# Another order of the first loads, and other transfers for h and D, in a kernel of a long convolution and a gated MLP

## The chip, the core and the metric

The kernel runs on one core of one Trainium2 chip. The core has a matrix engine (TensorE, PE in the profile; its weight loads are listed as PEld), a vector engine (VectorE, DVE), a scalar engine (ScalarE, ACT), GpSimd (POOL) and SyncE (SP), which here issues nearly all transfers. Every engine works through its own instructions in order and waits at semaphores for the others. The transfers themselves run on 16 DMA engines. The metric is device time in microseconds (us), lower is better: a median of 234.15 us over 3 runs before the change (233.83 to 234.19).

## The reference

One input x (2048 rows of 640) is normalised, and two branches of it are added to it:

```python
xn = layernorm(x)
# branch A: a short and a long convolution along the rows, gated by xn
k_shift = sum over t < 4 of (k shifted down by t rows) * shift_k[:, t]
kv = k_shift * v
y  = causal convolution of kv with ssm_k (length 2048 per column, by FFT) + kv * ssm_D
A  = xn * y
# branch B: a gated MLP of width 1728
h  = sigmoid(xn @ w_gate) * (xn @ w_up)
B  = h @ w_down
out = x + A + B
```

The data are bf16. In what follows h is the convolution's filter `A_ssm_k` (640 x 2048), not the MLP's hidden layer, which is called `hT`. D is `A_ssm_D`, 640 values.

## The kernel before

**Branch B** goes in four passes t of 512 rows, `xn` transposed in `xnT`. A pass makes 13 blocks of 128 hidden columns (5 matmuls of 512 columns for gate, 5 for up, L271), a 14th half block (L292), and then the product with the down weights `wd` (L315), in which each output tile takes 14 matmuls in two halves of 7. ScalarE makes the sigmoid (L280), VectorE the product into `hT` (L286), and VectorE adds the output to x (L320).

**Branch A** goes in five chunks c of 128 columns. The convolution is a transform in two stages, by matmuls with tables. For a chunk, VectorE makes kv from four shifted copies of k and the taps `sc` (`kv_op`, L348 to L357), and it brings the filter into the layout of kv by a transpose in 32 x 32 blocks (`h_turn`, L334, two per chunk, each over all 128 partitions of `hn`). D is added to the filter's first row by GpSimd (`add_D`, L328). Stage 1 are the matmuls L374 and L376, which write to `ps`; their results go through DRAM to be rearranged (L392 writes, L409 reads); stage 2 is L418; then come the products L431 and L433, and the way back (L447, L463, L479, L488). At the end `inv2_q` (L493) multiplies by xn into the small buffer `yx` and `inv2_x` (L498) adds it to x.

**Layernorm** of the rows of passes 1 to 3 (groups g) is made on the way: statistics (L200, L204), a power on GpSimd (L212), the normalised tile (L217 on VectorE, L229 on ScalarE). x of group 1 comes by `load_x` (L133).

**The order** of everything after the first blocks is written out by hand: a string `ORDER` of 841 letters (L659), each letter taking the next step of one chain. Chain `m` holds the first loads (L575 to L593) in the order in which SP issues them; the letters of `m` stand between those of the matmuls. So a load's place in that list sets its place in SP's queue. Within SP's queue every issue also waits for an earlier transfer: there are eight semaphores for transfers, used in turn, so the ninth transfer waits until the first has landed.

In chain `m` the order before is: gate and up weights of columns 512 to 1024, taps of chunk 0, a small table, gate and up weights 1024 to 1280, the first seven blocks of down weights, k of chunk 0 (two halo transfers, L163 and L164, and two halves, L159), gate and up weights from 1280 on, D and h of chunk 0, v of chunk 0 (L173), the other down weights, the table `S1t`, D and h of chunk 1, x of group 1, k and v of chunk 1.

**Buffers.** `hn` (the filter as loaded, 128 partitions x 4 x 512) exists once, so h of the next chunk can be issued only when both `h_turn` of the last one are done. D of a chunk goes to `dr` (1 x 128), also one buffer, which `add_D` reads. `sraw` (taps as loaded) and `yx` are two buffers of 1 KB per partition.

Partition 32q + r of `hn` holds, for k = 0 to 3, the q-th quarter (512 values) of row 32k + r of the chunk's filter.

Of the kernel before, what the change touches and what calls it, by code (L numbers as in the profile page):

```python
# [10 lines left out]
BF16 = mybir.dt.bfloat16  # L11
# [3 lines left out]
ALU = mybir.AluOpType  # L15

S = 2048
DM = 640
FF = 1728
P = 128  # L20
# [37 lines left out]
def kernel(  # L58
# [14 lines left out]
    nc = tc.nc  # L73
# [6 lines left out]
    Drow = A_ssm_D.rearrange("(o d) -> o d", o=1)  # L80
# [7 lines left out]
    res = ctx.enter_context(tc.tile_pool(name="res", bufs=1))  # L88
    cv = ctx.enter_context(tc.tile_pool(name="cv", bufs=1))
    dr = ctx.enter_context(tc.tile_pool(name="dr", bufs=1, space=bass.MemoryType.DRAM))  # L90
# [7 lines left out]
    S1t = res.tile([P, NB, 2, P], U16, name="S1t")  # L98
    TBt = res.tile([P, 2, NB, P], U16, name="TBt")
    SMt = res.tile([P, 3, 32], U16, name="SMt")  # L100
    S1 = S1t.bitcast(BF16)
    TB = TBt.bitcast(BF16)
    SM = SMt.bitcast(BF16)
# [21 lines left out]
    sync = nc.sync  # L125
# [3 lines left out]
    cin = [dict() for _ in range(NC)]  # L129
# [5 lines left out]
    def load_h(c):  # L135

        d = cin[c]
        d["hn"] = cv.tile([P, 4, 512], BF16, name="hn")
        d["dr"] = cv.tile([1, P], BF16, name="dr")
        sync.dma_start(d["dr"][:, :], Drow[:, c * P:(c + 1) * P])  # L140
        for q in range(4):
            src = A_ssm_k[c * P:(c + 1) * P, 512 * q:512 * q + 512].rearrange("(k r) t -> r k t", k=4)
            sync.dma_start(d["hn"][32 * q:32 * q + 32, :, :], src)

    def load_taps(c):
        cin[c]["sraw"] = cv.tile([P, 4 * P], BF16, name="sraw")
        sync.dma_start(cin[c]["sraw"][:], srow[:, 4 * c * P:4 * (c + 1) * P].to_broadcast((P, 4 * P)))

    def taps(c):
# [175 lines left out]

    def add_D(c):
        h0 = cin[c]["kvh"][0:1, 1, 0:2, :].rearrange("p b c -> p (b c)").rearrange("p (c e) -> p e c", e=2)[:, 0, :]
        nc.gpsimd.tensor_tensor(h0, h0, cin[c]["dr"][:, :], ALU.add)  # L328

    def h_turn(c, n):  # L330

# [27 lines left out]
    chunks = [dict() for _ in range(NC)]  # L359
# [6 lines left out]
    def st1_mm(c, n):  # L366
# [5 lines left out]
        for i in range(4):  # L372
            b = 4 * n4 + i
            nc.tensor.matmul(ps[:, i, 0:P], lhsT=S1[:, b, h, :], rhs=cin[c]["kvh"][:, 0, b, :], start=True, stop=True)  # L374
            hp = cin[c]["kvh"][:, 1, :, :].rearrange("p b c -> p (b c)").rearrange("p (b c e) -> p b e c", b=8, e=2)
            nc.tensor.matmul(ps[:, i, P:2 * P], lhsT=S1[:, b, h, :], rhs=hp[:, b // 2, b % 2, :], start=True, stop=True)  # L376

# [21 lines left out]
    def rd2(s):  # L399
# [5 lines left out]
        else:  # L405
            t2 = (xn[:, 12:NB, :].rearrange("p b d -> p (b d)")[:, 0:2048] if at == 2 else
                  S1[:, 8 * at:8 * at + 8, :, :].rearrange("p b h k -> p (b h k)")).rearrange("p (r e) -> p r e", r=8)
        src = chunks[c]["d1"].rearrange("(r q) h b e -> r (q h b) e", q=NQ)
# [60 lines left out]
    def rdb(c, n):  # L469
# [4 lines left out]
        elif c and n == 1:  # L474
            bi = S1[:, 8:NB, :, :].rearrange("p (h b) s c -> p h (b s) c", h=2)
        else:
# [12 lines left out]
                                 start=(h == 0), stop=(h == 1))  # L489

    def inv2_q(c, m):
        chunks[c]["yx", m] = yx = cv.tile([P, 4, P], BF16, name="yx")
        nc.vector.tensor_tensor(yx[:, :, :], chunks[c]["pb", m][:, :, :], xn[:, 4 * m:4 * m + 4, c * P:(c + 1) * P],  # L493
                                ALU.mult)

# [35 lines left out]
    for i in range(4):  # L531
        m = 3 if i < 3 else NC
# [15 lines left out]
    def step(k, fn, *args):  # L548
        chains[k].append((fn, args))
# [16 lines left out]
    def hs(c):  # L566
        return [(load_h, c)]

    def ks(c):
        return [(load_halo, c), (load_k, c, 0, 8), (load_k, c, 8, NB)]  # L570

    def vs(c):
        return [(load_v, c, 0, 8), (load_v, c, 8, NB)]

    for k in ((load_w, sync, 512, 1024, 0),  # L575
              (load_w, sync, 512, 1024, 1),
              (load_taps, 0),
              (sync.dma_start, SMt[:], SMd.ap()),
              (load_w, sync, 1024, 1280, 0),
              (load_w, sync, 1024, 1280, 1),  # L580
              (load_wd, sync, 0, 7),
              *ks(0),
              (load_w, sync, 1280, FF, 0),
              (load_w, sync, 1280, FF, 1),
              *hs(0),
              *vs(0),
              (load_wd, sync, 7, NFC),
              (sync.dma_start, S1t[:], S1d.ap()),
              *hs(1),
              (load_x, sync, 1),  # L590
              *ks(1),
              *vs(1)):
        step("m", *k)  # L593
# [4 lines left out]
    for c in range(NC):  # L598
        for n in range(2):
            step("H", h_turn, c, n)  # L600
        step("D", add_D, c)
        for n in range(8):
            step("a", st1_mm, c, n)
# [17 lines left out]
        for m in range(4):  # L621
            step("d", inv2_mm, c, m)
            step("q", inv2_q, c, m)
            step("q", inv2_x, c, m)
        for n in range(16):
            step("k", kv_op, c, n)
        if c == 0:
            continue
        step("T", load_taps, c)
        step("t", taps, c)  # L630
        if c > 1:
# [73 lines left out]
```

## Time and profile before

| what | value |
|---|---|
| median of 3 runs | 234.15 us (233.83 to 234.19) |
| profiled execution | 234.78 us |
| its span, first to last instruction | 233.0 us |
| VectorE busy | 203.4 us |
| ScalarE busy | 123.5 us |
| GpSimd busy | 12.4 us |
| bytes moved by DMA | 56.79 MB, 244 GB/s over the span |
| h loads (L143), issue to landing | 20 issues of 128 KB, 3.4 / 5.0 / 7.7 us (least, median, most) |
| x loads of a group (L133), median issue to landing | 7.0 us |

The shares in the profile are of the span. A digit in a line of slices stands for a fortieth of the span (5.8 us) and gives the busy share in tenths. In a timeline a row gives start and length in us, the engine, the line of the kernel and the operation, and in brackets the idle time of the engine before it with what ended it; SPq is the queue in which SP issues transfers, and the length there is that of the issue, not of the transfer. In a table of stretches, the columns after the stretch are its length, busy time (and instructions) of PE, PEld, DVE, ACT and POOL, TensorE's granted clock, the mean share of the DMA engines and GB/s. The DMA share counts the time of packets, which overlap, and so can be over 1.

### The profile page before, as it was taken

The page shows a single profiled execution, that of the slowest core. Times are in us where ns is not written, and L with a number is a line of the kernel's source. Part 1 is how long each engine was busy: PE and PEld are TensorE (multiplying, and loading weights), DVE is VectorE, ACT ScalarE, POOL GpSimd, SP SyncE. Part 2 cuts the span into 40 slices and gives each one's busy share as a digit, 9 for nine tenths or more (in the row PEclk, how much of TensorE's full clock was granted, in tenths as well). Part 3 has the DMA queues.
Part 4 walks back from the last instruction along what each step waited for, and adds up shares of the span by engine and source line. Part 5 has one row for each costly group of instructions (what it writes and reads, how often), then busy time and mean ns, then how long its engine had stood idle before and what let it go on. Part 6 is the DMA issues. An engine that isn't in the chain of part 4 may idle for free.

```text
span 233.0 us, 5431 instructions
## 1 busy us (share of the span) xinstructions
PE 227.5 (98%) x2199; PEld 130.9 (56%) x2200; DVE 203.4 (87%) x357; ACT 123.5 (53%) x158; POOL 12.4 (5%) x26
## 2 busy tenths in 40 slices
PE   7999999997999999999999999999999999999995
PEld 2844446776454555677554544478654544446772
DVE  5444899799999999999999999997799999997773
ACT  2533321676364887765675847674556667752000
POOL 5210010040001100000011000000000000000000
PEclk9999999999999999999999999999999999999999
DMA  6999999896999969999989899689989999364884
GB/s 199 325 329 208 267 317 294 208 266 143 330 221 303 299 221 242 263 223 230 329 237 277 224 319 272 184 217 190 269 210 311 279 263 254 117 169 117 220 266 136
DMA packets 96159, 56.79 MB, mean 244 GB/s; under 512 B 55878, under 2 KB 90374, under 8 KB 95878
## 3 DMA queue, kind: packets, MB, share of 16 engines
q1 hardware_dynamic: 95702, 56.03, 92.6%
q10 hardware_dynamic: 432, 0.41, 0.5%
q8 instruction: 17, 0.28, 0.5%
q14 instruction: 8, 0.07, 0.1%
HBM read 36.12 MB, written 18.35 MB: 234 GB/s over the span
## 4 chain that ended last, share of the span: by engine, by line
PE 87%; DVE 5%; DMA 4%; issue 1%; SPq 1%; ACT 0%; DVEq 0%
PE pu L271 22%; PE pg L271 22%; PE pd L315 21%; PE psb L488 4%; DMA x<-in_A_q_dram 4%; PE ps L374 3%; PE ps L376 3%; PE ps L418 3%; PE psa L447 2%; PE idle L514 2%; PE pg L292 1%; DVE st L200 1%; PE pg L262 1%; PE pu L262 1%; DVE acc L354 1%
## 5 line engine op out<-in xcount | busy, mean ns | idle before, releaser
L271 PEld LDWEIGHTS <-w 128*128 128x128 bf16 x500 | 46.7, 98 | 53.9 <-issue 4.3
L315 PE MATMUL pd<-wd,hT 128*128 128x320 bf16 (+2 forms) x447 | 65.9, 299 | 0.1
L271 PE MATMUL pu<-xnT,w 128*128 128x512 bf16 x250 | 62.2, 379 | 0.0
L271 PE MATMUL pg<-xnT,w 128*128 128x512 bf16 x250 | 62.2, 379 | 0.0
L315 PEld LDWEIGHTS <-hT 128*128 128x128 bf16 x448 | 41.7, 98 | 18.2 <-issue 2.4
L280 ACT ACTIVATE sig<-pg 128x512 bf16<-128x512 f32 x52 | 31.1, 601 | 30.5 <-PE pg L271 23.8
L286 DVE TENSOR_TENSOR hT<-sig,pu 128x512 bf16<-128x512 bf16 x52 | 35.0, 682 | 10.8 <-PE pu L271 6.9
L232 ACT CAST xz<-ps 128x1024 bf16<-128x1024 f32 x36 | 35.1, 1014 | 15.5 <-PE ps L418 15.5
L232 ACT CAST t<-ps 128x1024 bf16<-128x1024 f32 x24 | 23.8, 1012 | 16.7 <-PE ps L376 14.5
L433 DVE TENSOR_TENSOR xz<-xz 128x2048 bf16<-128x2048 bf16 x20 | 24.4, 1221 | 0.2
L374 PE MATMUL ps<-kvh,S1t 128*128 128x128 bf16 x160 | 21.5, 218 | 1.2 <-DVE kvh L357 1.2
L376 PE MATMUL ps<-kvh,S1t 128*128 128x128 bf16 x160 | 21.6, 220 | 0.0
L354 DVE TENSOR_TENSOR acc<-acc,tmp 128x1024 bf16<-128x1024 bf16 x30 | 20.5, 684 | 0.3
L352 DVE TENSOR_TENSOR tmp<-kx,sc 128x1024 bf16<-128x1024 bf16 x30 | 20.5, 682 | 0.3
L320 DVE TENSOR_TENSOR x<-pd,x 128x320 bf16<-128x320 f32 (+2 forms) x32 | 15.2, 484 | 3.8 <-PE pd L315 3.6
L374 PEld LDWEIGHTS <-S1t 128*128 128x128 bf16 x160 | 15.5, 97 | 3.9 <-DVE kvh L357 1.4
L376 PEld LDWEIGHTS <-S1t 128*128 128x128 bf16 x160 | 15.4, 96 | 2.7 <-issue 0.2
L200 DVE BATCH_NORM_STATS2 st<-x 128x6 f32<-128x320 bf16 x32 | 13.8, 473 | 2.3 <-DMA x<-in_A_q_dram 2.3
L232 ACT CAST TBt<-ps 128x1024 bf16<-128x1024 f32 x14 | 13.8, 1012 | 2.7 <-PE ps L376 2.7
L493 DVE TENSOR_TENSOR yx<-psb,xn 128x512 bf16<-128x512 f32 x20 | 13.7, 687 | 1.4 <-PE psb L488 0.8
L431 DVE STREAM_SHUFFLE xz<-xz 128x512 f32<-128x512 f32 x20 | 14.6, 729 | 0.0
L232 ACT CAST ao<-psa 128x1024 bf16<-128x1024 f32 x9 | 9.0, 1013 | 8.6 <-PE psa L447 6.9
(56 smaller groups left out, 159.2 us busy)
## 6 DMA issues: line engine op xcount, KB each, us to landing
t<-d SPq DMA_DIRECT2D x15, 512.0 KB, 6.0
d<-t SPq DMA_DIRECT2D x13, 512.0 KB, 4.1
d<-TBt SPq DMA_DIRECT2D x7, 512.0 KB, 5.9
d<-ao SPq DMA_DIRECT2D x6, 512.0 KB, 5.5
bi<-d SPq DMA_DIRECT2D x6, 512.0 KB, 5.4
kx<-in_A_k_dram SPq DMA_DIRECT2D x10, 256.0 KB, 5.8
hn<-in_A_ssm_k_dram SPq DMA_DIRECT2D x20, 128.0 KB, 5.0
kvh<-in_A_v_dram SPq DMA_DIRECT2D x10, 256.0 KB, 5.2
```

The costliest lines, as they stand in the source:

```text
L200: nc.vector.bn_stats(st[:, i, SD * s2:SD * s2 + SD], x[:, b, s2 * 320:(s2 + 1) * 320])
L232: nc.scalar.copy(out=out, in_=in_)
L271: nc.tensor.matmul(pg[:, :], lhsT=w[:, c, u * UP + fc * P:u * UP + (fc + 1) * P], rhs=xnT[:, :, c, :], start=(c == 0), stop=(c == NC - 1))
L280: nc.scalar.activation(sig[fc][:, :], pgs[0, fc][:, :], ACT.Sigmoid)
L286: nc.vector.tensor_tensor(hT[:, fc, :], sig[fc][:, :], pgs[1, fc][:, :], ALU.mult)
L315: nc.tensor.matmul(pd[:, :], lhsT=hT[:, fc, bb * P:(bb + 1) * P], rhs=wd[:, fc, es], start=(fc == 0), stop=(fc == NFC - 1))
L320: nc.vector.tensor_tensor(x[:, 4 * t + bb, es], pds[bb, half][:, :], x[:, 4 * t + bb, es], ALU.add)
L352: nc.vector.tensor_tensor(d["tmp"][:, :, :], kx[:, lo + 3 - m:hi + 3 - m, :], sb(m), ALU.mult)
L354: nc.vector.tensor_tensor(d["acc"][:, :, :], d["acc"][:, :, :], d["tmp"][:, :, :], ALU.add)
L374: nc.tensor.matmul(ps[:, i, 0:P], lhsT=S1[:, b, h, :], rhs=cin[c]["kvh"][:, 0, b, :], start=True, stop=True)
L376: nc.tensor.matmul(ps[:, i, P:2 * P], lhsT=S1[:, b, h, :], rhs=hp[:, b // 2, b % 2, :], start=True, stop=True)
L433: nc.vector.tensor_tensor(z[:, 1:3, :, :], z[:, 0:1, :, :].to_broadcast((P, 2, 8, P)), z[:, 1:3, :, :], ALU.mult)
```

## The change

Chain `m` gets another order: k of chunk 0 stands ahead of the gate and up weights 1024 to 1280; the first seven blocks of down weights go behind v of chunk 0; x of group 1 stands ahead of h of chunk 1. Four transfers of h per chunk remain, but each now takes 32 whole rows of the filter (one k) and writes 1 KB into each of the 128 partitions, where before each took one quarter of 128 rows and wrote 4 x 1 KB into each of 32 partitions. The layout in `hn` is the same. D comes once, 640 values in one transfer ahead of chunk 0's h, into a buffer `Dt` of its own. To make room, `sraw` and `yx` share one buffer under the tag `sy`.

```diff
+    Dt = res.tile([1, DM], BF16, name="Dt")
...
     def load_h(c):
         d = cin[c]
+        if c == 0:
+            sync.dma_start(Dt[:, :], Drow[:, :])
         d["hn"] = cv.tile([P, 4, 512], BF16, name="hn")
-        d["dr"] = cv.tile([1, P], BF16, name="dr")
-        sync.dma_start(d["dr"][:, :], Drow[:, c * P:(c + 1) * P])
-        for q in range(4):
-            src = A_ssm_k[c * P:(c + 1) * P, 512 * q:512 * q + 512].rearrange("(k r) t -> r k t", k=4)
-            sync.dma_start(d["hn"][32 * q:32 * q + 32, :, :], src)
+        for k in range(4):
+            r0 = c * P + 32 * k
+            sync.dma_start(d["hn"][:, k, :], A_ssm_k[r0:r0 + 32, :].rearrange("r (q t) -> q r t", q=4))
...
-        cin[c]["sraw"] = cv.tile([P, 4 * P], BF16, name="sraw")
+        cin[c]["sraw"] = cv.tile([P, 4 * P], BF16, name="sraw", tag="sy")
...
-        nc.gpsimd.tensor_tensor(h0, h0, cin[c]["dr"][:, :], ALU.add)
+        nc.gpsimd.tensor_tensor(h0, h0, Dt[:, c * P:(c + 1) * P], ALU.add)
...
-        chunks[c]["yx", m] = yx = cv.tile([P, 4, P], BF16, name="yx")
+        chunks[c]["yx", m] = yx = cv.tile([P, 4, P], BF16, name="yx", tag="sy")
...
               (sync.dma_start, SMt[:], SMd.ap()),
+              *ks(0),
               (load_w, sync, 1024, 1280, 0),
               (load_w, sync, 1024, 1280, 1),
-              (load_wd, sync, 0, 7),
-              *ks(0),
               (load_w, sync, 1280, FF, 0),
               (load_w, sync, 1280, FF, 1),
               *hs(0),
               *vs(0),
+              (load_wd, sync, 0, 7),
               (load_wd, sync, 7, NFC),
               (sync.dma_start, S1t[:], S1d.ap()),
+              (load_x, sync, 1),
               *hs(1),
-              (load_x, sync, 1),
               *ks(1),
               *vs(1)):
```

## The prediction

> **What bounds the kernel now.** I read the page's busy shares first, then the waits of TensorE, then the timelines of the engine that it waits for, and last the queue of transfers behind that.
>
> ```profile
> PE 227.5 (98%) x2199; PEld 130.9 (56%) x2200; DVE 203.4 (87%) x357; ACT 123.5 (53%) x158; POOL 12.4 (5%) x26
> PEclk9999999999999999999999999999999999999999
> DMA  6999999896999969999989899689989999364884
> PE ps L374 <- DVE kvh L357: 1.2, 1, 1.2
> PE idle L514 <- DVE st L121: 1.2, 1, 1.2
> ```
>
> TensorE (PE) is busy 98% of the span at the full granted clock, and between its first instruction and the end it waits once: 1.2 us for VectorE (DVE). So the work on TensorE sets the time, a change of loads can win little more than those 1.2 us, and it can lose any amount by making TensorE wait. What decides the one wait is in the timeline of VectorE (start, length, what ran; in brackets the idle time before it and who ended it), then that of TensorE, then the chain of waits:
>
> ```profile
> 42.79 1.11 DVE L334 STREAM_TRANSPOSE kvh<-hn 128x512 f32<-128x512 f32 x1 [1.15 <-DMA hn<-in_A_ssm_k_dram]
> 44.29 0.89 DVE L200 BATCH_NORM_STATS2 st<-x 128x6 f32<-128x320 bf16 x2 [0.39 <-DMA x<-in_A_q_dram]
> 54.49 0.69 DVE L357 TENSOR_TENSOR kvh<-acc,kvh 128x1024 bf16<-128x1024 bf16 x1
> ...
> 55.24 0.23 PE L374 MATMUL ps<-kvh,S1t 128*128 128x128 bf16 x1 [1.20 <-DVE kvh L357]
> ...
> 35.46 8.80 DMA x<-in_A_q_dram
> ```
>
> VectorE takes chunk 1's h (`h_turn(1, 0)`, L334) at 42.79 after 1.15 us of waiting for its load, then the first statistics of x's second group at 44.29 after 0.39 us more; from there it runs without a gap to the product L357 at 54.49 that TensorE waits for. Two landings, h(1) and x(1), therefore set this stage: each microsecond that both come later is one on the path, since TensorE has no other wait in which to give it back. VectorE works in order, so all behind L334 (statistics, taps of k, the evictions L320) stands still with it.
>
> Where the transfers stand: the queue of SP, and the mean throughput of stretches.
>
> ```profile
> 22.76 1.76 SPq L143 DMA_DIRECT2D hn<-in_A_ssm_k_dram  x4
> 29.85 0.58 SPq L673 DMA_DIRECT2D S1t<-tabS  x1
> 33.67 1.75 SPq L143 DMA_DIRECT2D hn<-in_A_ssm_k_dram  x4
> 35.46 1.29 SPq L133 DMA_DIRECT2D x<-in_A_q_dram  x1
> ...
> 27.00:29.40 2.40, 2.40 (x13) 1.08 (x11) 2.20 (x4) 0.60 (x1) 0.00 (x0) 1.00 1.24 212
> 31.60:34.30 2.70, 2.70 (x14) 1.26 (x13) 2.67 (x5) 0.60 (x1) 0.48 (x1) 1.00 1.11 362
> 34.30:36.70 2.40, 2.40 (x13) 1.09 (x12) 2.37 (x5) 0.60 (x1) 0.00 (x0) 1.00 0.97 385
> ```
>
> The last number of the lower rows is GB/s: 212 while h(0) moves (1 KB rows into 32 partitions), 362 while the second down weights move (1.25 KB rows into 128 partitions), 385 while the table S1 moves. The DMA engines are backlogged from 10 to 45 us, so a transfer lands when the engines have worked off all that stands ahead of it.
>
> **How many engines carry a transfer.** The trace's semaphore increments show it. Loads with an outermost dimension of 128, 112 or 32 on both sides get 16 increments as data land (first h of chunk 0: 26.91 to 27.55). The halo L164 with 15 partitions gets one at 16.20, as its issue ends (16.06), and 15 later (19.31 to 21.50). D's L140, one partition, gets one at 32.54, as it has been issued, and one at 37.56: one engine. So a transfer is cut along its outermost dimension. The new h load has 128 partitions as destination, but its source is laid out as 4 pieces of a row x 32 rows x 512; the source's outermost dimension is 4. A cut into equal shares of both sides has 4 shares. No row of before shows two sides that differ, so the bounds are 4 engines and 16; I take 4, since every row follows the outermost count.
>
> [...]
>
> **The change, part by part.**
>
> 1. *h in four transfers of 128 partitions.* Same 512 KB and the same 512 rows of 1 KB per chunk. Before, 16 engines take 2.45 us (landings 26.91 to 29.37). With 4 engines each has 128 KB instead of 32. Rate of one engine, from the three stretches: 212/16 = 13.3 GB/s (9.9 us a chunk), 362/16 = 22.6 (5.8 us), 385/16 = 24.1 (5.4 us). I take 22.6, the row nearest in row size and spread: 5.8 - 2.45 = +3.35 us per chunk on those four engines (bounds +2.95 and +7.4).
>
> 2. *x(1) ahead of h(1).* VectorE still wants h(1) first, and now h(1) is the last of the two. Bytes ahead of the pair's end are the same as before. The median engine ended x(1) at 41.5 (16 increments, 41.13 to 44.27). The four engines end h(1) at 41.5 + 2 x 3.35 = 48.2 (both h(0) and h(1) are ahead of it). L334 then starts at 48.2, the statistics at 48.2 + 1.11 + 0.03 = 49.3 instead of 44.29: +5.0 us. The last engine of x(1) (44.27) no longer counts; an engine is 2.6 us behind there, after a 16 KB instruction fetch at 35.36, and it need not be one of the four.
>
> 3. *k(0) ahead of the weights and down weights.* VectorE got k(0) at 22.14 after 0.57 us of waiting; those are gone, but the next products (L286) wait for TensorE, 0.57 us at 25.20: worth 0. Gate and up weights from column 1024 are wanted at 24.9 and those from 1280 at 29.25; without 1120 KB of down weights ahead (3.3 us, 15.3 to 18.5) both come in time.
>
> 4. *First down weights behind v(0).* On the four engines h(0) ends at 29.37 - 3.25 + 3.35 = 29.5 (wanted 30.12), v(0) at 31.7 (first half 30.6, wanted 31.15), the first down weights at 35.0 (wanted 36.80), the second at 38 (wanted at 36.80 + 14 x 0.136 = 38.7), S1 at 40.4 + 0.3 (wanted 40.54): 0 by small margins. A miss there of up to 1 us lies ahead of the wait at 55 and is swallowed by it.
>
> 5. *D in one transfer.* Four issues (0.23 to 0.91 us of SP each) and the wait of SP for GpSimd (1.6 us ahead of L140) go. h(1) still waits for `h_turn(0, 1)`, which ends at 33.65, so its issue is not earlier: 0.
>
> 6. *Shared buffer of taps and `yx`.* The last copy of taps starts at 109.5 and the first `yx` (L493) at 145.9: no wait, 0.
>
> 7. *h of chunks 2 to 4.* Landing before at 69.42, 92.44, 112.14; wanted at 72.14, 96.02, 119.68. With +3.35: 0.6 late, 0.2 and 4.2 early. v of chunk 2 behind it (73.57, wanted 75.8) would be 1.1 late. I take +0.7 for chunk 2 (0 to 3), 0 for the rest.
>
> Sum: +5.0 + 0.7 = +5.7 us. The profiled execution took 234.78 us (span 233.0 and 1.78 around it), so 240.5; it stands 0.6 above the runs' median of 234.15, from which the forecast is 239.9 us.
>
> **Rivals.**
>
> - *Four engines, cheap* (0.20): while the other twelve are done, the four run at 24 to 27 GB/s for h and for what stands behind it. h(1) at about 46.5, statistics 47.6: +3.3, nothing in chunk 2: 237.4 us.
> - *Four engines, dear* (0.17): 1 KB rows cost more than the 1.25 KB row says, 18 GB/s: 7.3 us a chunk, h(1) at 51.2, +8.0, and chunk 2 +2: 244.2 us. The 13.3 GB/s stretch speaks for it; it is one where 16 engines write into 32 partitions.
> - *Sixteen engines, and 128 partitions are quicker than 32* (0.09; the other side, faster): at 362 GB/s h takes 1.45 us, 1.0 less per chunk. The pair then ends on the slowest engine at 44.27 - 2.0 = 42.3, L334 starts there and the statistics at 43.4, 0.85 earlier: 233.3 us. It decides if h(1) lands before 43.1. For it speaks 212 against 362 GB/s; against it that the source's outermost count is 4. [...]
> - *Sixteen engines at the old rate* (0.09): the order alone remains. h(1) ends at 44.3, transposes, statistics at 45.4: +1.1, 235.2 us; with part of the quicker h, no change.
>
> **How the numbers follow.** The forecast itself has 0.45. Four engines make 0.82, and none of its cases is within 0.2% (0.5 us), about what this kernel's runs can tell from no change. Of the sixteen-engine cases 0.18, some 0.08 are faster by more than that, 0.05 within, 0.05 slower. So faster 0.08, same 0.05, slower 0.87. Four engines alone give 236.5 to 245; to take in part of the order-only case the range is 235.0 to 245.0, which leaves out some 0.13 below and 0.05 above.
>
> **What would show it.** In the new profile h's loads get 5 increments, not 16, and take over 5 us from first to last of a chunk; L334 at 42.79 has an idle time of 5 to 7 us before it, ended by hn; the wait of L374 grows from 1.2 to about 6 us; k's wait at L348 is gone; D's L140 stands once. Wrong: 16 increments per h load; or TensorE's new waits lie elsewhere, at the down weights or S1.

## The result, and the profile after

The changed kernel took 244.41 us (243.09 to 244.99, 6 runs) beside 234.34 us for the kernel before in the same runs: a ratio of 1.0423 with a 95% interval of 1.0385 to 1.0461, so 9.9 us slower (9.0 to 10.8). Ratios, here and below, leave out runs that stand apart from the others of their kernel: one of the kernel before (336.42 us), one of e5 (242.94) and one of e12 (242.30). The direction and the range of the prediction held; the forecast of 239.9 was 4.5 us short of the median.

The profiled execution took 243.09 us with a span of 241.3, which is 8.3 us more than before; it is the quickest of the six runs, while the profiled execution before is slower than the median of its runs, so the profiles show somewhat less than the medians. First the page's busy shares and the granted clock in slices, then the waits of TensorE (us in total, times, longest):

```profile
PE 231.2 (96%) x2199; PEld 132.4 (55%) x2200; DVE 203.3 (84%) x357; ACT 123.2 (51%) x158; POOL 12.5 (5%) x26
PEclk9999999979999999999999999999999999999999
```

```profile
PE ps L375 <- ACT t L233: 3.3, 1, 3.3
...
PE pg L272 <- ACT sig L281: 0.9, 1, 0.9
PE ps L419 <- ACT ao L233: 0.5, 1, 0.5
PE ps L375 <- DVE kvh L358: 0.5, 1, 0.5
...
```

No engine got more work: VectorE, ScalarE and GpSimd are busy as long as before. TensorE, with the same 2199 matmuls, is busy 3.7 us longer (231.2 against 227.5), and its idle time is 4.6 us longer (10.1 against 5.5): together the 8.3 us. Of the 3.7 us, 0.7 lie in the first ten us, where executions differ, 1.65 in a stretch at half clock (the ninth slice has 0.7; see the end), and about 1.1 behind 111 us. Two of the new waits (L375) belong to one stage, between 50 and 60 us; the others (`sig`, `ao`) belong to a later stage, which the prediction does not have.

The first stage, in the timeline of VectorE and then in that of TensorE:

```profile
48.24 1.10 DVE L335 STREAM_TRANSPOSE kvh<-hn 128x512 f32<-128x512 f32 x1 [5.94 <-DMA hn<-in_A_ssm_k_dram]
49.26 0.84 DVE L201 BATCH_NORM_STATS2 st<-x 128x6 f32<-128x320 bf16 x2
...
101.93 2.10 DVE L335 STREAM_TRANSPOSE kvh<-hn 128x512 f32<-128x512 f32 x2 [0.90 <-DMA hn<-in_A_ssm_k_dram]
```

```profile
50.30 0.22 PE L375 MATMUL ps<-kvh,S1t 128*128 128x128 bf16 x1 [3.25 <-ACT t L233]
...
60.16 0.23 PE L375 MATMUL ps<-kvh,S1t 128*128 128x128 bf16 x1 [0.53 <-DVE kvh L358]
...
131.06 1.24 PE L272 MATMUL pg<-xnT,w 128*128 128x512 bf16 x5 [0.92 <-ACT sig L281]
...
135.91 0.66 PE L419 MATMUL ps<-xn,SMt 32*32 32x512 bf16 x16 [0.54 <-ACT ao L233]
```

VectorE stands idle for 5.94 us until chunk 1's h has landed, and the statistics begin at 49.26 instead of 44.29, 4.97 us later. What follows on TensorE is not one wait of about 6 us before the first matmul on chunk 1's kv, as the prediction had it: 3.25 us come at 50.30, for ScalarE's cast into `t`, and only 0.53 at 60.16. ScalarE's timeline has the reason for the first:

```profile
48.68 0.66 ACT L156 COPY sc<-sraw 128x512 bf16<-128x512 bf16 x1 [4.34 <-DMA sraw<-in_A_shift_k_dram]
49.24 1.92 ACT L233 CAST t<-ps 128x1024 bf16<-128x1024 f32 x2
```

The taps of chunk 1 are loaded behind h(1), and the casts stand behind their copy in ScalarE's order. The copy began at 44.75 before.

How the loads landed is seen in the semaphore increments. Each h load has five: one from SP as it is issued, four as data land. The last increments (us):

```
           before         after
h(0)       29.37          24.69  26.18  27.64  29.21   (the four loads)
x(1)       41.13-44.27    41.08-42.27  (the 16 increments)
h(1)       42.66          43.64  45.13  46.76  48.11   (the four loads)
h(2)       69.42          77.11   (last of four)
h(3)       92.44          101.74   (last of four)
h(4)       112.14         124.43   (last of four)
```

One load of 128 KB takes 1.5 us on four engines, 32 KB each, so about 22 GB/s per engine. The prediction had 22.6, and 48.2 for the landing that came at 48.11.

Taking the same matmul in both traces, and the time at which it ran before, TensorE is 4.9 us late at 55 us and still at 111, then 5.3, 5.9 at 123, 7.0 at 124, 8.0 at 128 and 8.25 at the end. So 4.9 us are lost by chunk 1's h, and 3.3 us more, nearly all of them between 111 and 128, which is 116 to 136 in the trace after. There the timeline of ScalarE, after, and then its counterparts before:

```profile
124.57 1.01 ACT L233 CAST TBt<-ps 128x1024 bf16<-128x1024 f32 x1 [0.70 <-PE ps L377]
129.50 1.01 ACT L233 CAST t<-ps 128x1024 bf16<-128x1024 f32 x1 [3.92 <-DVE xz L432]
130.40 1.09 ACT L281 ACTIVATE sig<-pg 128x512 bf16<-128x512 f32 x2
...
134.85 1.01 ACT L233 CAST ao<-psa 128x1024 bf16<-128x1024 f32 x1 [1.91 <-DMA d<-ao]
```

```profile
120.61 1.01 ACT L232 CAST t<-ps 128x1024 bf16<-128x1024 f32 x1 [0.51 <-PE ps L376]
121.52 0.60 ACT L280 ACTIVATE sig<-pg 128x512 bf16<-128x512 f32 x1
...
126.04 1.01 ACT L232 CAST ao<-psa 128x1024 bf16<-128x1024 f32 x1
```

The cast into `t` waits 0.51 us before, for TensorE, and 3.92 us after. It comes 8.89 us later than before, where the cast ahead of it (124.57) is 5.48 us late: 3.4 us are lost here. The releaser named, `xz` on VectorE, is the latest that the profile saw; the write of an earlier `t` to DRAM (L393) had its last increment at 129.40, 0.10 us before the cast, and three of the experiments name that write at the same place. Before the change, the write in this place of SP's queue had landed at 116.96, 3.65 us ahead of the cast. Behind the cast, in ScalarE's order, stand two sigmoids, and TensorE waits 0.92 us for them at 131.06. Why that write is late shows in its increments and those of its neighbours:

```
transfer behind h(4)   first 12 engines   last 4 engines
h(4), four loads       -                  118.98 120.79 122.60 124.43 (last of each)
next                   121.67-122.49      125.81-125.83
next                   123.10-123.69      127.14-127.17
next                   124.67-125.00      128.15-128.18
write of t             126.89-127.11      129.37-129.40
next                   127.98-128.38      130.12-130.14
```

Four engines carry all of h; twelve engines are done with each following transfer 1.8 to 3.5 us sooner than they. A transfer over 16 engines has landed when the last four are done, so all of these are late. Part of the lateness is older than h(4): the transfers that stand in SP's queue between h(3) and h(4) landed 6.9 to 9.4 us later than before, while TensorE was 4.9 us late, and the last one ahead of h(4), of `xn` into `xnT`, at 117.48 instead of 108.13. ScalarE shows it at 116.95, where it waits 2.38 us for the taps of chunk 4; before, it had no wait there. In the trace before no transfer over 16 engines between 85 and 136 us is split in such a way: its 16 increments are at most 1.8 us apart, and there is no group of four behind.

### The profile page after: what moved, and what is told of

Same layout as the page of the kernel before. It is cut to its first block, busy times and chain, and to the rows that moved or that the text cites. A ratio compares the mean times of both kernels' runs of the same rounds, so it can differ in the third digit from the quotient of the medians.

```text
span 241.3 us, 5425 instructions
## 1 busy us (share of the span) xinstructions
PE 231.2 (96%) x2199; PEld 132.4 (55%) x2200; DVE 203.3 (84%) x357; ACT 123.2 (51%) x158; POOL 12.5 (5%) x26
## 4 chain that ended last, share of the span: by engine, by line
PE 54%; DMA 17%; DVE 15%; SPq 5%; issue 4%; ACT 2%; POOL 1%; DVEq 0%; ACTq 0%; POOLq 0%
PE pu L272 14%; PE pg L272 13%; PE pd L316 13%; DMA hn<-in_A_ssm_k_dram 7%; PE psb L489 4%; DMA x<-in_A_q_dram 3%; DMA d<-ao 3%; DVE st L201 3%; DMA kvh<-in_A_v_dram 3%; DVE kvh L335 3%; PE ps L419 2%; SPq L144 2%; PE psa L448 2%; DVE tmp L353 2%; DVE acc L355 2%
## 5 line engine op out<-in xcount | busy, mean ns | idle before, releaser
L316 PE MATMUL pd<-wd,hT 128*128 128x320 bf16 (+2 forms) x447 | 67.2, 303 | 0.1
L316 PEld LDWEIGHTS <-hT 128*128 128x128 bf16 x448 | 42.3, 99 | 18.8 <-issue 2.4
L375 PE MATMUL ps<-kvh,S1t 128*128 128x128 bf16 x160 | 21.9, 220 | 3.8 <-ACT t L233 3.3
L377 PE MATMUL ps<-kvh,S1t 128*128 128x128 bf16 x160 | 22.0, 222 | 0.0
L375 PEld LDWEIGHTS <-S1t 128*128 128x128 bf16 x160 | 15.6, 98 | 3.8 <-DVE kvh L358 1.5
L335 DVE STREAM_TRANSPOSE kvh<-hn 128x512 f32<-128x512 f32 x10 | 10.9, 1098 | 6.8 <-DMA hn<-in_A_ssm_k_dram 6.8
```

Of the source, the lines that this page charges most:

```text
L316: nc.tensor.matmul(pd[:, :], lhsT=hT[:, fc, bb * P:(bb + 1) * P], rhs=wd[:, fc, es], start=(fc == 0), stop=(fc == NFC - 1))
L335: nc.vector.transpose(to[:, 4 * n:4 * n + 4, :, :], hv[:, 4 * n:4 * n + 4, :, :])
```

## The experiments

Every kernel was timed beside the kernel before on the same chip. In the table each ratio is turned into us by 234.2; the ratios' intervals are with the runs below. How late TensorE is in an experiment is again read at the same matmul, and the times given for it are those of the kernel before.

| kernel | h in the new form for chunks | order of loads | us against before |
|---|---|---|---|
| after | 0 to 4 | new | +9.9 (9.0 to 10.8) |
| e1 | none | new | +1.6 (0.9 to 2.3) |
| e7 | none | new, but x(1) behind h(1) | +1.1 (0.4 to 1.8) |
| e10 | none | only k(0) and down weights moved | +1.3 (0.8 to 1.9) |
| e2 | 0 to 4 | old | +9.9 (8.5 to 11.3) |
| e4 | 0, 1 | new | +6.3 (5.4 to 7.1) |
| e5 | 2, 3, 4 | new | +4.2 (3.3 to 5.1) |
| e6 | 4 | new | +1.3 (0.6 to 1.9) |
| e11 | 3 | new | +2.7 (1.5 to 3.9) |
| e12 | 3, 4 | new | +4.8 (3.6 to 5.9) |
| e8 | chunk 1 on two engines | new | +8.5 (7.7 to 9.3) |
| e3 | 0 to 4, on 16 engines | new | -0.2 (-0.5 to 0.1) |
| e9 | none; D once, shared buffer | old | +0.2 (-0.3 to 0.7) |

**e1: the change with the old h transfers.**

```diff
-        for k in range(4):
-            r0 = c * P + 32 * k
-            sync.dma_start(d["hn"][:, k, :], A_ssm_k[r0:r0 + 32, :].rearrange("r (q t) -> q r t", q=4))
+        for q in range(4):
+            src = A_ssm_k[c * P:(c + 1) * P, 512 * q:512 * q + 512].rearrange("(k r) t -> r k t", k=4)
+            sync.dma_start(d["hn"][32 * q:32 * q + 32, :, :], src)
```

> The changed kernel with the h transfers of before (a quarter of 128 rows into 32 partitions each); order, D and the shared buffer stay changed. Theory (the four-engine transfers of h cost all of it): 16 increments per h load, the idle time ahead of h_turn of chunk 1 is 1 to 2.5 us because h(1) now stands behind x(1), 234.0 to 235.5 us. Rival (the order costs: down weights late, x ahead of h): 239 us or more. Rival (shared buffer or D): well over 235.5 with new waits at yx or the taps.

Measured: 235.37 us (234.49 to 237.81), 1.0068 [1.0039, 1.0097], and 16 increments per h load. The h transfers are the bulk of the loss; but with these transfers something of the rest costs about 1.6 us, where the prediction had nothing.

**e2: the kernel before with the new h transfers alone.** The edit is the reverse of e1's, in the kernel before.

```diff
-        for q in range(4):
-            src = A_ssm_k[c * P:(c + 1) * P, 512 * q:512 * q + 512].rearrange("(k r) t -> r k t", k=4)
-            sync.dma_start(d["hn"][32 * q:32 * q + 32, :, :], src)
+        for k in range(4):
+            r0 = c * P + 32 * k
+            sync.dma_start(d["hn"][:, k, :], A_ssm_k[r0:r0 + 32, :].rearrange("r (q t) -> q r t", q=4))
```

> The kernel before with only the h transfers changed (order, D per chunk and buffers as before). Theory: 5 increments per h load, about 5.9 us of transfer per chunk; h(1) ends at about 46, x(1) behind it at about 48, and the loss in chunk 4 is there too: 242 to 245 us. Rival (order): at most 235 us.

Measured: 243.80 us (242.90 to 245.51), 1.0423 [1.0364, 1.0481]: the whole loss, without a change of order. In VectorE's timeline of this kernel, h(0) is late too, and after h(1) comes x(1):

```profile
33.10 1.11 DVE L334 STREAM_TRANSPOSE kvh<-hn 128x512 f32<-128x512 f32 x1 [2.35 <-DMA hn<-in_A_ssm_k_dram]
47.93 1.10 DVE L334 STREAM_TRANSPOSE kvh<-hn 128x512 f32<-128x512 f32 x1 [3.32 <-DMA hn<-in_A_ssm_k_dram]
49.62 0.89 DVE L200 BATCH_NORM_STATS2 st<-x 128x6 f32<-128x320 bf16 x2 [0.59 <-DMA x<-in_A_q_dram]
```

TensorE is 5.5 us late at 55 us and 9.5 at the end: again two parts, here 5.5 and 4.0.

**e3: the same four transfers, the source's rows outermost.** The source's outermost count is then 128 instead of 4. The quarters of the filter come to lie in other partitions, so this kernel convolves with a permuted filter and is no replacement as it stands; its instructions and sizes are those of the change.

```diff
-            sync.dma_start(d["hn"][:, k, :], A_ssm_k[r0:r0 + 32, :].rearrange("r (q t) -> q r t", q=4))
+            sync.dma_start(d["hn"][:, k, :], A_ssm_k[r0:r0 + 32, :].rearrange("r (q t) -> (r q) t", q=4))
```

> The changed kernel with h still in four transfers into all 128 partitions, but partition 4r+q takes quarter q of row r, so that source and destination both have an outermost count of 128; the filter then lies permuted in the partitions, and the convolution is made with that permuted filter. All instructions and sizes stay. Theory (the count of 4 on the source side): 16 increments per load, 1.4 to 2.5 us per chunk, 233.3 to 235.5 us. Rival (1 KB pieces into 128 partitions are slow as such, or the order costs): 240 us or more.

Measured: 233.80 us (233.54 to 234.09), 0.9990 [0.9977, 1.0003], 16 increments. The issues of h (least, median, longest ns) after and in e3, then e3's VectorE where h(1) was waited for:

```profile
L144 SPq DMA_DIRECT2D hn<-in_A_ssm_k_dram x20: 522/618/2947, 19.3 to 115.0; - x20
```

```profile
L144 SPq DMA_DIRECT2D hn<-in_A_ssm_k_dram x20: 328/432/937, 19.4 to 106.8; - x20
```

```profile
41.99 1.10 DVE L335 STREAM_TRANSPOSE kvh<-hn 128x512 f32<-128x512 f32 x1
43.02 0.84 DVE L201 BATCH_NORM_STATS2 st<-x 128x6 f32<-128x320 bf16 x2
```

The bytes, the 1 KB rows, the 128 partitions and the order are those of the change; only the source's outermost count differs (and with it which partition gets which quarter), and the loss is gone. So is the wait before L335 (1.15 us before the change, 5.94 after it). A load of 128 KB lands 0.4 us behind the last one (first increments of h(0) at 23.68, 24.05, 24.42, 24.87), against 1.5 us in the changed kernel. TensorE keeps 1.4 us of waits in this execution, 1.0 less than before the change, and it ends 1.07 us earlier than in the profile before. By the medians (233.80 against 234.05) little of that is left, since the execution profiled before (234.78) is near the top of its runs; the interval still holds 1. Beside e1, which has the same order, e3 is 1.6 us faster by the medians: the 1.6 us that e1 loses are not lost where h comes quickly on 16 engines.

**e4 and e5: the new h for the first two chunks, and for the last three.** In both, the loop of the change stands under a condition, and the old one under `else`; e5 has `c > 1`.

```diff
+        if c < 2:
+            for k in range(4):
+                r0 = c * P + 32 * k
+                sync.dma_start(d["hn"][:, k, :], A_ssm_k[r0:r0 + 32, :].rearrange("r (q t) -> q r t", q=4))
+        else:
+            for q in range(4):
...
```

> The changed kernel with the new h transfers for chunks 0 and 1 only and those of before for chunks 2 to 4. Theory (two losses: about 5 us where chunk 1's h lands late, the rest at chunks 3 and 4): the idle time ahead of h_turn of chunk 1 stays about 5.9 us, the later delays go, 238.5 to 240.5 us. Rival (all of the loss follows from the early stage, the later part only shifts with it): 243 to 245 us.

> The changed kernel with the h transfers of before for chunks 0 and 1 and the new ones for chunks 2 to 4. Theory (two separate losses): no stall at chunk 1, about 1 us at chunk 3's h_turn and about 3 us more around the filter of chunk 4; with the 1.3 us that the order alone showed, 238 to 240 us. Rival (the late loss needs the early stall): 234.5 to 236.5 us.

Measured: e4 240.10 us (239.53 to 241.40), 1.0268 [1.0231, 1.0305]; e5 239.28 us (238.39 to 242.94), 1.0179 [1.0140, 1.0217]. In e4 TensorE is 4.7 us late at 55 us and stays so to the end. Its waits:

```profile
PE ps L380 <- ACT t L238: 3.0, 1, 3.0
PE ps L380 <- DVE kvh L363: 2.3, 1, 2.3
...
```

In e5 TensorE is 0.9 us late at 55 us, 1.7 at 111, 3.7 at 124 and 4.9 at the end, and for the cast into `t` the write of `t` is named:

```profile
126.18 1.01 ACT L238 CAST t<-ps 128x1024 bf16<-128x1024 f32 x1 [4.36 <-DMA d<-t]
```

The two losses stand apart: chunk 1's h costs 4.7 us over e1 (6.3 - 1.6), the h of chunks 2 to 4 costs 2.6 us over e1 by the ratios (4.2 - 1.6) and 4.0 by TensorE's delay in this trace.

**e6, e11 and e12: which of the late chunks.** The same edit with `c == 4`, `c == 3` and `c > 2`.

```diff
+        if c == 4:
```

> The changed kernel with the new h transfers for chunk 4 only. Theory (the four engines are late with all that stands behind chunk 4's filter, so that writes and reads between the stages land late): about 2 to 3 us over the kernel with all h transfers of before, 236.5 to 238.5 us. Rival (chunk 4's filter is early enough, and the late loss is what chunks 2 and 3 left behind): at most 1 us over it, 235 to 236.3 us.

> The changed kernel with the new h transfers for chunk 3 only. Theory (the late loss comes from the backlog of four engines that adds up over two or three chunks): about 1 us over the kernel with all h transfers of before (235.4), 235.6 to 237 us. Rival (chunk 3 alone brings nearly all of the late 4 us): 238 us or more.

> The changed kernel with the new h transfers for chunks 3 and 4. Theory (the backlog adds up, chunk 4's load stands behind what chunk 3's has delayed): 238 to 239.5 us. Rival (each chunk costs for itself, chunk 4 nothing): as with chunk 3 alone, within 0.7 us of that kernel.

Measured: e6 235.38 us (234.82 to 237.63), 1.0054 [1.0026, 1.0082], no more than e1. So my first account, by which chunk 4's h next to the write of `t` does it alone, fell. e11 took 237.19 us (236.05 to 238.84), 1.0116 [1.0066, 1.0166], a little more than was expected of it; e12 239.41 us (237.75 to 242.30), 1.0203 [1.0154, 1.0253]. The same cast into `t` in e6, e11 and e12:

```profile
120.52 1.01 ACT L238 CAST t<-ps 128x1024 bf16<-128x1024 f32 x1 [0.51 <-PE ps L382]
```

```profile
124.22 1.01 ACT L238 CAST t<-ps 128x1024 bf16<-128x1024 f32 x1 [1.20 <-DMA d<-t]
```

```profile
124.13 1.01 ACT L238 CAST t<-ps 128x1024 bf16<-128x1024 f32 x1 [4.16 <-DMA d<-t]
```

The last increment of the write of `t`, and the start of this cast, say why two chunks do more than either alone. In the table, extra lateness is lateness against the kernel before, less that of the cast just ahead of this one on ScalarE; so it is only what is lost here:

| kernel | h in the new form for | write of `t` landed | cast begins | extra lateness of the write | extra lateness of the cast |
|---|---|---|---|---|---|
| before | none | 116.96 | 120.61 | - | - |
| e6 | 4 | 120.34 | 120.52 | 3.5 | 0 |
| e11 | 3 | 124.12 | 124.22 | 4.2 | 0.7 |
| e12 | 3, 4 | 124.03 | 124.13 | 7.2 | 3.7 |
| e5 | 2, 3, 4 | 126.08 | 126.18 | 7.4 | 3.8 |
| after | 0 to 4 | 129.40 | 129.50 | 7.0 | 3.4 |
| e2 | 0 to 4, old order | 130.30 | 130.40 | 6.2 | 2.6 |

In the last five kernels the cast begins 0.10 us behind the write. In the kernel before the write had 3.65 us to spare. Chunk 4's h alone makes it 3.5 us later, which uses nearly all of that margin and costs nothing; chunk 3's alone makes it 4.2 us later, and the two together 7.2, nearly the sum, of which the margin is taken off only once. In e12 the write is split as in the changed kernel (twelve engines at 121.53 to 121.85, four at 123.99 to 124.03). In e11 it is not (123.65 to 124.12), so lateness that h(3) caused is there handed on to transfers over all engines; by which step of the queue was not taken apart. By TensorE's delay behind 55 us the late loss is 0 in e6, 1.9 us in e11 and 3.4 in e12; by the ratios over e1 it is none, 1.1 and 3.2.

**e7 and e10: what e1 lost.** e7 is e1 with x(1) behind h(1) again. e10 is the kernel before with k(0) ahead of the weights and the first down weights behind v(0), nothing else.

```diff
               (sync.dma_start, S1t[:], S1d.ap()),
-              (load_x, sync, 1),
               *hs(1),
+              (load_x, sync, 1),
```

```diff
               (sync.dma_start, SMt[:], SMd.ap()),
+              *ks(0),
...
-              (load_wd, sync, 0, 7),
-              *ks(0),
...
               *vs(0),
+              (load_wd, sync, 0, 7),
               (load_wd, sync, 7, NFC),
```

> The changed kernel with the h transfers of before and with x of group 1 behind h of chunk 1 again; k and the down weights stay in their new places, D and the shared buffer too. Theory (x ahead of h is what the order costs): 233.7 to 234.5 us, as before the change. Rival (the down weights' place, D or the shared buffer cost it): 235 to 236 us.

> The kernel before with only k of chunk 0 moved ahead of the gate and up weights and the first down weights behind v (D, buffers, h and x as before). Theory (the place of k and the down weights is what lost about 1 us in the kernels with all h transfers of before): 235 to 236 us, with runs spread over 2 us or more. Rival: 233.7 to 234.6 us.

Measured: e7 235.41 us (233.90 to 236.98), 1.0047 [1.0018, 1.0076]; e10 235.49 us (234.76 to 236.04), 1.0057 [1.0035, 1.0079]. The order of x(1) and h(1) is not it; the order of k(0) and the down weights alone costs as much as all of e1. (That e10's runs would spread over 2 us or more was wrong: they spread over 1.3.) Where on the way is less clear. In no profile of e1, e7 or e10 does TensorE lose time between 9 and 46 us. e10's VectorE:

```profile
43.03 1.11 DVE L334 STREAM_TRANSPOSE kvh<-hn 128x512 f32<-128x512 f32 x1 [0.99 <-DMA hn<-in_A_ssm_k_dram]
44.66 0.89 DVE L200 BATCH_NORM_STATS2 st<-x 128x6 f32<-128x320 bf16 x2 [0.52 <-DMA x<-in_A_q_dram]
```

The statistics are 0.37 us later than before the change, and the rest of the 1.3 us isn't seen in this one execution. The five profiles that have the new order and the old h for chunk 1 (e1, e5, e6, e11, e12) begin that transposition at 42.99, 44.17, 43.20, 45.39 and 42.76: the same loads end on a slowest engine that differs by 2.6 us. In e11, at 45.39, one engine had its last increment at 45.27, the first one at 42.15. TensorE takes the difference over: at 55 us it is 1.2 us later in e5 and 2.4 in e11 than in e1. A loss that is in some executions and not in others would look so; why an engine is late there was not followed further.

**e8: chunk 1's h on two engines.** Eight loads of 64 partitions with a source whose outermost count is 2; the other chunks as before.

```diff
+        if c == 1:
+            for hf in range(2):
+                for k in range(4):
+                    r0 = c * P + 32 * k
+                    src = A_ssm_k[r0:r0 + 32, 1024 * hf:1024 * hf + 1024].rearrange("r (q t) -> q r t", q=2)
+                    sync.dma_start(d["hn"][64 * hf:64 * hf + 64, k, :], src)
```

> The changed kernel with the h transfers of before, except chunk 1: eight transfers of 64 partitions, each from a source with an outermost count of 2. Theory (the smallest outermost count sets the number of engines): 3 increments per transfer (two engines and the issuer's own), 256 KB per engine at about 22 GB/s, 12 us from x(1) at about 39 to about 51; h_turn of chunk 1 at 50 to 52, statistics 7 to 8.5 us later than before, 241 to 243 us. Rival (all engines share whatever the source's shape): 16 increments and at most 236 us.

Measured: 242.79 us (242.35 to 243.67), 1.0362 [1.0330, 1.0395], three increments per load (one at the issue, two as data land), 1.35 to 1.60 us from one load to the next, the last at 50.84. VectorE, then TensorE's wait:

```profile
50.92 1.10 DVE L342 STREAM_TRANSPOSE kvh<-hn 128x512 f32<-128x512 f32 x1 [9.04 <-DMA kx<-in_A_k_dram]
...
```

```profile
PE ps L382 <- ACT t L240: 6.2, 1, 6.2
...
```

The releaser named is k, but h's last increment lies 0.08 us ahead of the start. Sixteen (e3), four and two engines give h(1) at 41.54, 48.11 and 50.84. A 64 KB load on two engines takes about as long as a 128 KB load on four (1.35 to 1.63 us in the changed kernel): 32 KB per engine in both.

**e9: D once, and the shared buffer.** The kernel before with these two edits.

```diff
+        if c == 0:
+            sync.dma_start(Dt[:, :], Drow[:, :])
...
-        cin[c]["sraw"] = cv.tile([P, 4 * P], BF16, name="sraw")
+        cin[c]["sraw"] = cv.tile([P, 4 * P], BF16, name="sraw", tag="sy")
...
-        chunks[c]["yx", m] = yx = cv.tile([P, 4, P], BF16, name="yx")
+        chunks[c]["yx", m] = yx = cv.tile([P, 4, P], BF16, name="yx", tag="sy")
```

> The kernel before with D in one transfer and the buffer shared by taps and yx, and nothing else (order and h transfers of before). Theory (these two cost nothing): 233.7 to 234.6 us, the ratio's interval holds 1. Rival (they are what the kernel with all h transfers of before lost, about 1 us): 235 to 236 us.

Measured: 234.21 us (233.72 to 235.24), 1.0010 [0.9989, 1.0030]: no difference that can be told.

## Why the prediction was right, and where it fell short

**Bound, direction, engines: right.** Four engines carry each h load (five increments), TensorE's waits set the end, and without the four engines (e3) the loss is gone. That a source count of 4 makes it four was my estimate, from loads whose two sides have the same count. It held: with source counts of 4 (the changed kernel), 128 (e3) and 2 (e8), the h loads had 5, 16 and 3 increments, of which one of the 5 and one of the 3 came from SP at the issue.

**Items 1 and 2, chunk 1: right in size.** Predicted 22.6 GB/s per engine, h(1) at 48.2, statistics at 49.3, +5.0 us; measured about 22, 48.11, 49.26 and +4.97. The way there agrees within 0.8 us: the last of the four engines was done with h(0) at 29.21 (29.5 predicted), with v(0) at 30.93 (31.7) and with the table S1 at 40.62 (40.7). The chain from there held: TensorE was 4.9 us late in the changed kernel, and e4 costs 4.7 us over e1. What was not foreseen is that the taps, queued behind h(1), hold up ScalarE as well and so bring 3.25 us of the wait forward; it adds nothing, since VectorE would have been waited for as long.

**Items 3 and 4, k(0) and the down weights: predicted 0; +1.3 us with the old h transfers (e10; e1 and e7 agree), and not to be told in the changed kernel.** The page showed every transfer of that stretch in time by margins of a few tenths, and I took in-time as free. In the changed kernel TensorE loses nothing between 7 and 46 us (it is 0.67 us late at both), and e2, without the new order, loses the same 9.9 us. So no run shows that this order costs anything beside the late h, as item 4 allowed, nor that it costs nothing. Where the 1.3 us of e10 lie stays open.

**Items 5 and 6: right.** e9 finds nothing.

**Item 7, h of chunks 2 to 4: the step that failed.** It was sized at +0.7 us, all of it at chunk 2; it is 2.6 us by e5 against e1, and 3.3 (the changed kernel) to 4.0 (e2, e5) by TensorE's delay, none of it at chunk 2: TensorE stays 4.9 us late from 55 us to 111, in the times of the kernel before. I asked when each chunk's own h is wanted, and by that measure the answer was near: the only wait for h there is 0.90 us on VectorE, at 101.93. What I left out is the work behind h on the same four engines. Each chunk's h comes later against the delayed work than the one ahead of it: h(2) landed 7.69 us later, h(3) 9.30 and h(4) 12.29, which is 2.8, 4.4 and 7.0 us more than the 4.9, 4.9 and 5.3 us by which TensorE was late, where I had +3.35 for each. The transfers over 16 engines that follow are as late as the slowest four, among them the write of `t`, whose buffer ScalarE wants back; in its order the sigmoids follow, then TensorE. The price was to be had from the trace before: that write landed 3.65 us ahead of the cast, so one chunk at +3.35 is free, and two that add up, 6.7, are about 3 us too late. The cast lost 3.4 in the changed kernel and 3.7 in e12.

**The sum.** In the changed kernel's trace the loss has two parts, 4.9 us at chunk 1 and 3.3 at the late chunks, where 5.0 and 0.7 were predicted. By the ratios, chunk 1 costs 4.7 us over e1 and the late chunks 2.6, and with e1's own 1.6 that makes 8.9 us, against 9.9 (9.0 to 10.8) measured and 5.7 predicted. Such a sum takes the parts as independent, which they need not be: e2, with the old order, loses as much with 5.5 us at chunk 1 and 4.0 at the late chunks.

**The rivals.** The dear one, at 244.2 us, has the right number by luck, as it comes there by another way: it had 18 GB/s, h(1) at 51.2 and +8.0 us in chunk 1. e8, where h(1) does land at 50.84, shows what that is like: the statistics at 51.94, 7.65 us late, and TensorE late by 7.6 from there to the end. In the changed kernel h(1) was three microseconds sooner, and the rest came at the other end of the kernel. The rate of 18 GB/s did come up, later: h(4)'s loads are 1.81 us apart, 32 KB per engine. The cheap one, at 237.4 us, had 24 to 27 GB/s per engine; in the trace before, 385 GB/s from 34.3 to 36.7 us and 434 from 35 to 36 us are 24.1 and 27.1 for each of 16 engines, and each of the four moved h(0) and h(1) at about 22. The sixteen-engine rival with 128 partitions, put at 233.3 us, is e3 in all but the layout: 233.80. Its quicker load was measured there (0.4 us per load into 128 partitions, in place of 0.6 into 32 before), though no run shows why; its condition, 16 engines, was not met by this source (five increments per load). The order-only rival, 235.2 us, is e1 with 235.37; but its reason, h(1) behind x(1), fell with e7.

## What to carry to other kernels

Before a load is rearranged, look at the outermost count on both its sides and, in the trace, at the number of its increments: with counts of 4 and 2 on the source's side, all bytes went over four and two engines (5 and 3 increments). Price such a load by everything that queues behind it on those engines, not only by its own user, since every transfer over all engines lands with the slowest of them (behind h(4) the last four engines were done 1.8 to 3.5 us after the other twelve). For each of these transfers, read from the trace how long it had landed before it was wanted: here lateness up to that margin was free (3.5 us of 3.65 in e6), lateness from two loads added up (3.5 and 4.2 us alone, 7.2 together in e12), and the rest was lost (3.7 us at e12's cast). In this kernel, whose matrix engine is busy 98% of the time, moving loads had little to win (e3, -0.2 us), and the landing that this engine already waited for passed its delay on nearly in full (4.97 us became 4.9).

## What was not expected of the hardware

- The loads on four engines also take longer to issue: 522 to 2947 ns each on SP, median 618, against 328 to 937 and 432 in e3. Four of them held SP's queue for 5.64 us where it had been 1.75:

```profile
31.11 0.66 SPq L134 DMA_DIRECT2D x<-in_A_q_dram  x1
34.34 5.64 SPq L144 DMA_DIRECT2D hn<-in_A_ssm_k_dram  x4
```

- TensorE's clock fell with a long wait, and in the changed kernel only after it, when TensorE was already working again. In the table of stretches for the changed kernel, and then for e8 (the column behind GpSimd's is the clock):

```profile
...
50.00:54.00 4.00, 3.70 (x28) 2.80 (x28) 3.86 (x13) 3.09 (x4) 0.51 (x1) 0.69 1.21 233
```

```profile
...
50.00:56.00 6.00, 3.14 (x20) 2.34 (x20) 4.94 (x14) 3.49 (x4) 0.00 (x0) 0.50 0.97 224
```

  The trace's record of the clock has half speed for 3.41 us in the changed kernel (51.54 to 54.95), after a wait of 3.25 us that ended at 50.30; for 3.41 us in e2 (52.49 to 55.90), after a wait of 3.01 us; for 6.83 us in e8, from inside a wait of 6.22; and not at all in the profile of e4, after 3.05. So the length of the wait alone does not decide it. Up to the end of the work, the lengths in the records are whole multiples of 3.41 us (in the changed kernel 44.37 is 13 of them and 187.73 is 55, before the change 228.69 is 67). If the time is cut into such stretches from the record's first entry on, TensorE was idle for 2.17 us of the stretch just ahead of the fall in the changed kernel, 2.53 in e2 and 2.75 in e8; in e4 the wait falls on two stretches, and 1.91 us is the most in one. Two of e4's four runs have a mean clock of 0.993, where the six of the changed kernel have 0.986 to 0.993, and two have 1.0; what sets them apart was not shown, since the traces of the two with 0.993 were not kept. Beside VectorE's delay the slow clock cost little: e4's profile, with the same late h(1) and the full clock, has TensorE 4.7 us late at 55 us, the changed kernel 4.9.
